# Eleven instead of seven products of zeros ahead of the first real matrix product

## The chip, the cores and the metric

The kernel runs on one NeuronCore of one Trainium2 chip. The metric is the device time of one execution in microseconds (us). The time before is the median of three executions, 374.33 us (373.33 to 376.72). Engines are named as the profile names them: PE is TensorE's matmul, PEld its load of the stationary operand, DVE is VectorE, ACT is ScalarE, POOL is GpSimd, and SP is SyncE, which issues most transfers.

## What is computed

The reference mixes two branches of one input x (1 x 2048 x 512) with a gate per row:

```python
g = sigmoid((x * gate_w).sum(-1, keepdims=True))
a = irfft2(rfft2(x) * (w_r + 1j * w_i))          # over both axes, 2048 x 512
b = gelu(x @ w1 + b1) @ w2 + b2                  # 512 -> 1792 -> 512
return g * a + (1 - g) * b
```

Everything is float32; both branches read the same x.

## The kernel before

**Tiling.** The 2048 rows are handled as 16 row groups of 128, and the 512 columns as four blocks of 128 (the index q in the code). The Fourier branch is a product with tables over columns (tiles pd), a product with tables over rows (py), vector butterflies, the filter, and the way back (pz, pa). The MLP runs over four blocks of 512 columns of transposed input (c) and two halves of the 14 hidden blocks (f): `ph` is the first layer's accumulator (12 products per hidden block: 4 blocks q times 3), `po` the second layer's.

**Split operands.** Each float32 operand of a real product is split into a high part and a low part (names ending in h and l: `wa0h`, `wa0l` for the first layer's weights of hidden block 0, `mxh`, `mxl` for the input, `g_0h`, `g_0l` for GELU's result, `wb0h`, `wb0l` for the second layer). ACT or DVE makes the high part as a rounded copy, DVE the low part as a difference. For some weights the low part is made in another way: ACT writes minus the high part (L557), and a transfer issued by POOL adds the raw weights from memory on top (L495). High times high, high times low and low times high are accumulated.

**Order.** Every piece of work is a step of a graph (`add`, with an engine, an estimated cost and a rank from a table). A planner (`Graph.schedule`) runs through the graph with these costs once, when the kernel is built, and so fixes the order of instructions on each engine. On the chip each engine works its list in order, and waits on semaphores for what it needs from the others.

**The start.** DVE clears a 128 x 128 tile `zero` (L568). PE then multiplies it with itself, as 128 x 512 products into a tile `none` that nobody reads (`warm`, through the helper `mm`, L504). In the meantime the first input blocks (`xf`) and first-layer weights (`war`) come from memory. ACT copies the first input block's high part in two halves (L637), DVE that of the second block (L639), the weights' first halves come from DVE (L1059) and ACT (L1057). The first eight real products are 128 x 128 wide and go to hidden block 0 (`ph`); then follow groups of four 128 x 256 wide products that alternate between hidden blocks 0 and 1, then the first Fourier products `pd`, which need ACT's `eoh` (L699), DVE's `eol` (L701) and the gate columns that DVE writes into the table `cf` (L612, L613). With its last product, hidden block 0 goes to ACT for GELU (L1125), then to `g_0h` (ACT, L551) and `g_0l` (DVE, L552).

The product of zeros, as the code gives it:

```python
zero, none = buf("hid", [P, P], F32R, "zero"), buf("pm", [P, 4, P], F32, "none", pool=pp)
mm(none.ap(), zero.ap(), bcast(zero.ap(), 4), True, True)
```

Of the kernel before, what the change touches and what calls it, by code (L numbers as in the profile page):

```python
# [264 lines left out]
class Graph:  # L265
# [5 lines left out]
    def add(self, eng, cost, lag, emit, reads=(), writes=(), rank=1):  # L271

        s = Step(len(self.steps), eng, cost, lag, emit, [], rank)
        deps = set()

        def parts(x):
            b, p = x if isinstance(x, tuple) else (x, None)
            if isinstance(b, View):
                return b.buf, range(b.lo, b.lo + b.n) if p is None else (b.lo + p,)
            return b, range(len(b.wrote)) if p is None else (p,)  # L280

        for x in reads:
            b, ps = parts(x)
            for p in ps:
                if b.wrote[p] is not None:
                    deps.add(b.wrote[p])
                b.read[p].append(s)
            if b not in s.bufs:
                s.bufs.append(b)
        for x in writes:  # L290
            b, ps = parts(x)
            for p in ps:
                if b.wrote[p] is not None:
                    deps.add(b.wrote[p])
                deps.update(b.read[p])
                b.wrote[p], b.read[p] = s, []
            if b not in s.bufs:
                s.bufs.append(b)
        deps.discard(s)
        for d in deps:  # L300
            d.after.append(s)
        s.need = s.open = len(deps)
        for b in s.bufs:
            b.left += 1
            if b.seq is None:
                b.seq = self.order.get(b.cls, 0)
                self.order[b.cls] = b.seq + 1
        self.steps.append(s)
        return s
# [125 lines left out]
def tile_kernel(ctx: ExitStack, tc: tile.TileContext, xt, xc, w1, w2, b1, b2, x0g, wf, wrev, out, consts):  # L435
# [10 lines left out]
    vec, act, pe, sp = nc.vector, nc.scalar, nc.tensor, nc.sync  # L446
# [7 lines left out]
    add = g.add  # L454

    def buf(tag, shape, dt=F32, name="", parts=1, pool=None, cls=None):
        slots.setdefault(tag, 1)
        return Buf(g, pool or (sb if tag in whole else sc), tag, shape, dt, name, parts, cls)
# [44 lines left out]
    def mm(ps, w, x, start, stop):  # L503
        pe.matmul(ps, w, x, start=start, stop=stop)  # L504
# [6 lines left out]
    def bcast(ap, *ns):  # L511
        return bass.AP(tensor=ap.tensor, offset=ap.offset, ap=[list(ap.ap[0]), *[[0, n] for n in ns], list(ap.ap[1])])
# [54 lines left out]
    zero, none = buf("hid", [P, P], F32R, "zero"), buf("pm", [P, 4, P], F32, "none", pool=pp)  # L567
# [3 lines left out]
      -1).table = "gelu"  # L571

    def warm():
        for _ in range(7):
            mm(none.ap(), zero.ap(), bcast(zero.ap(), 4), True, True)

    add("pe", 3.9, 0.1, warm, [zero], [none], 0)


    x0 = buf("ba", [P, NQ, P], F32, "xf0", parts=2)  # L580
# [718 lines left out]
```

## Time and profile before

| what | value |
|---|---|
| three executions | 373.33, 374.33, 376.72 us |
| the profiled execution's own time | 375.85 us |
| its span, first to last instruction | 374.0 us |
| instructions | 5583 |
| PE matmuls, of which products of zeros | 1850, 7 |
| transfers | 61.20 MB, mean 164 GB/s |

The profiled execution is 1.5 us longer than the median of the three; 1.85 us of its time lie outside its span. Busy shares in the profile are of the whole span; here only the first 50 us matter for the change, and those are read from the rows of the timeline and from the table by stretches. Times in rows count from the first instruction. Starts of products that follow each other are the measure of how fast PE works, since a product's own duration contains the pipeline behind it.

### The profile page before, as it was taken

What the parts mean: (1) busy time and instruction counts of PE and PEld (TensorE: products, weight loads), DVE (VectorE), ACT (ScalarE), POOL (GpSimd) and SP (SyncE); (2) the same over time, 40 slices, a digit from 0 to 9 for tenths busy, and PEclk for the clock granted to TensorE, in tenths of its full rate; (3) what the DMA queues carried; (4) which work ended last, traced back from release to release, by engine and by line L of the source; (5) the groups of instructions that cost most, each with busy time, mean ns of one, the idle gap of its engine ahead of it and who ended that gap; (6) DMA issues with size and microseconds to landing.
All of it is one profiled execution on the core that took longest, in us unless ns stands there. A gap on an engine that the chain in (4) does not pass through costs nothing.

```text
span 374.0 us, 5583 instructions
## 1 busy us (share of the span) xinstructions
PE 367.2 (98%) x1850; PEld 313.4 (84%) x1850; DVE 337.2 (90%) x745; ACT 225.7 (60%) x415; POOL 34.0 (9%) x54
## 2 busy tenths in 40 slices
PE   8999899999999999999999999999999999999996
PEld 6988788888888888888888888888888888888885
DVE  5799899999999999999999897789698999999982
ACT  4799757679935622357297429852964599544500
POOL 0023000000000000003024010100020000001110
PEclk9999999999999999999999999999999999999999
DMA  8999987286875153388778881325242053365456
GB/s 256 330 276 243 219 261 254 79 266 190 263 227 150 31 189 126 123 232 162 175 203 143 183 252 45 48 60 224 42 63 44 2 194 124 91 184 140 105 166 181
DMA packets 41909, 61.20 MB, mean 164 GB/s; under 512 B 4656, under 2 KB 22384, under 8 KB 41104
## 3 DMA queue, kind: packets, MB, share of 16 engines
q1 hardware_dynamic: 36120, 50.62, 42.4%
q0 software_dynamic: 5472, 9.96, 17.2%
q8 instruction: 14, 0.23, 0.3%
q10 hardware_dynamic: 288, 0.26, 0.2%
q14 instruction: 15, 0.12, 0.1%
HBM read 41.82 MB, written 16.92 MB: 157 GB/s over the span
## 4 chain that ended last, share of the span: by engine, by line
PE 89%; DMA 4%; ACT 3%; issue 1%; DVE 1%; POOL 0%; ACTq 0%; SPq 0%; POOLq 0%
PE po L504 40%; PE ph L504 38%; PE pz L504 4%; PE pa L504 3%; PE py L504 2%; PE pd L504 2%; DMA wb4l<-in_w 2%; DMA wbr<-in_w 1%; DMA xf<-in_x0g 1%; ACT ph L1125 1%; ACT eoh L699 0%; POOL wb3l L495 0%; DVE mxl L642 0%; ACT zb L740 0%; ACT wa6l L557 0%
## 5 line engine op out<-in xcount | busy, mean ns | idle before, releaser
L1125 ACT ACTIVATE ph<-ph,b1t 128x512 f32<-128x512 f32 x56 | 36.9, 658 | 51.0 <-PE ph L504 50.7
L958 ACT ACTIVATE sw<-y,al 64x512 f32<-64x512 f32 x32 | 22.8, 722 | 3.2 <-DVE y L821 2.6
L917 DVE TENSOR_TENSOR m<-y,wf 128x514 f32<-128x514 f32 x32 | 20.8, 689 | 0.1
L504 PE MATMUL py<-zb,tf 128*128 128x258 f32 x96 | 17.1, 287 | 0.0
L965 DVE SCALAR_TENSOR_TENSOR pq<-y,al,sw 128x256 f32<-128x256 f32 x32 | 14.5, 483 | 2.6 <-ACT sw L961 2.4
L773 ACT ACTIVATE y<-pys 64x257 f32<-64x257 f32 x32 | 13.4, 418 | 5.1 <-DVE pys L770 4.6
L504 PEld LDWEIGHTS py<-zb,tf 128*128 128x128 f32 x96 | 14.8, 190 | 1.4
L1164 ACT ACTIVATE o<-po,b2t 128x512 f32<-128x512 f32 x8 | 5.5, 688 | 16.3 <-PE po L504 16.3
L495 POOL DMA_DIRECT2D w<-ba x8 | 7.0, 873 | 77.8 <-ACT v4h L551 44.9
L504 PEld LDWEIGHTS pa<-zb,ci 128*128 128x128 f32 x96 | 13.0, 191 | 0.9
L694 DVE TENSOR_TENSOR w<-eo 128x256 f32<-128x256 f32 x32 | 13.2, 420 | 0.2
L742 DVE TENSOR_TENSOR zb<-pd,zb 128x256 fp32r<-128x256 f32 x32 | 12.6, 419 | 0.8 <-PE py L504 0.4
L504 PE MATMUL pa<-zb,ci 128*128 128x256 f32 x96 | 13.2, 283 | 0.0
L746 DVE TENSOR_TENSOR zb<-zb,pd 128x256 fp32r<-128x256 f32 (+1 forms) x32 | 12.8, 412 | 0.3
L691 DVE TENSOR_TENSOR eo<-xf 128x256 f32<-128x256 f32 x32 | 13.0, 419 | 0.0
L495 POOL DMA_DIRECT2D bacc<-o x8 | 7.0, 873 | 64.5 <-ACT o L1168 58.0
L740 ACT ACTIVATE zb<-pd 128x256 fp32r<-128x256 f32 x32 | 11.1, 382 | 2.5 <-PE pd L504 2.2
L495 POOL DMA_DIRECT2D wa7l<-in_w x1 | 0.9, 875 | 125.9 <-ACT wa7l L557 125.9
L701 DVE TENSOR_TENSOR eol<-w,eoh 128x512 fp32r<-128x512 f32 (+1 forms) x17 | 11.1, 655 | 1.2 <-ACT eoh L699 1.2
L986 DVE TENSOR_TENSOR zb<-pz,zb 128x512 fp32r<-128x512 f32 x16 | 11.0, 688 | 0.2
L988 DVE TENSOR_TENSOR zb<-zb,pz 128x512 fp32r<-128x512 f32 x16 | 11.0, 687 | 0.2
L1168 ACT ACTIVATE o<-po 128x512 f32<-128x512 f32 x8 | 4.7, 592 | 9.7 <-PE po L504 9.7
(558 smaller groups left out, 1309.9 us busy)
## 6 DMA issues: line engine op xcount, KB each, us to landing
wf<-in_wf SPq DMA_DIRECT2D x16, 257.0 KB, 3.5
bacc<-o SPq DMA_DIRECT2D x16, 256.0 KB, 3.2
xf<-in_xt SPq DMA_DIRECT2D x14, 256.0 KB, 4.9
wbr<-in_w SPq DMA_DIRECT2D x14, 256.0 KB, 4.5
war<-in_w SPq DMA_DIRECT2D x13, 256.0 KB, 3.1
xm<-in_xc SPq DMA_DIRECT2D x12, 256.0 KB, 4.8
tf<-tf SPq DMA_DIRECT2D x16, 192.0 KB, 4.3
bb<-bacc SPq DMA_DIRECT2D x8, 256.0 KB, 4.5
```

What stands on the lines that cost most here:

```text
L495: return add("pool", 2.3 * kb / 340, 3.4, lambda: nc.gpsimd.dma_start(dst(), src(), accum_op=ALU.add), reads, writes, rank)
L504: pe.matmul(ps, w, x, start=start, stop=stop)
L691: v(lambda s=s, op=op: vec.tensor_tensor(eo.ap()[:, s], x.ap()[:, 0:2], x.ap()[:, 2:4], op=op), 256, [x], [(eo, s)], feed)
L694: v(lambda s=s, op=op: vec.tensor_tensor(w.ap()[:, s], eo.ap()[:, :, 0], eo.ap()[:, :, 1], op=op), 256, [eo], [(w, s)], feed)
L701: v(lambda k=k: vec.tensor_tensor(l.ap()[:, k], w.ap()[:, k], h.ap()[:, k], op=ALU.subtract), 256 * len(ps), sub[0] + sub[1], sub[2], feed)
L742: v(lambda c=c: vec.tensor_tensor(segs(xl, c, 0, P + c), segs(ps, c, P, P + 4), segs(xh, c, 0, P + c), op=ALU.subtract), 256, [(ps, c), xh ...
L746: v(lambda o=o, i=i: vec.tensor_tensor(xl.ap()[:, :, o], xl.ap()[:, :, o], ps.ap()[:, :, i], op=ALU.add), 256, [ps], [xl], 0)
L773: a(lambda o=o, i=i: act.activation(Y[j].ap()[o:o + HP, 1], pys.ap()[i:i + HP, 1], AF.Copy), 257, [(pys, 1)], [(Y[j], 1 + k)], 0, more=0.1)
L917: v(lambda mk=mk, k=k, y=y, w=w: vec.tensor_tensor(mk.ap(), y.ap(), w.ap()[:, k:k + 1, :ND].to_broadcast([P, 2, ND]), op=ALU.mult), 514, [ ...
L958: a(lambda sw=sw, y=y, o=o, i=i: act.activation(sw.ap()[o:o + HP], y.ap()[i:i + HP, ::-1, :HD], AF.Copy, scale=al.ap()[i:i + HP, 0:1]), 51 ...
L965: v(lambda sw=sw, pq_=pq_, y=y, j=j, k=k, op=op: vec.scalar_tensor_tensor(pq_.ap()[:, k], y.ap()[:, k, :HD], al.ap()[:, 1 + j:2 + j], sw.a ...
L1125: a(lambda f=f, ps=ps: act.activation(ps.ap(), ps.ap(), AF.Gelu_apprx_tanh, bias=b1t.ap()[:, f:f + 1]), 600, [b1t], [ps], 0.9 if half else ...
```

## The change

`warm` issues eleven products of zeros instead of seven, and the cost by which the planner reckons this step rises from 3.9 to 4.35 us.

```diff
     def warm():
-        for _ in range(7):
+        for _ in range(11):
             mm(none.ap(), zero.ap(), bcast(zero.ap(), 4), True, True)
 
-    add("pe", 3.9, 0.1, warm, [zero], [none], 0)
+    add("pe", 4.35, 0.1, warm, [zero], [none], 0)
```

PE's list begins with the zeros, followed by the first products of hidden blocks 0 and 1. Before:

```order
L504 MATMUL none<-zero 128x512 x7
L504 MATMUL ph_0_132<-mxh_121,wa0h 128x128 x8
L504 MATMUL ph_0_132<-mxl_128,wa0h 128x256 x4
L504 MATMUL ph_1_172<-mxh_121,wa1h 128x256 x4
L504 MATMUL ph_1_172<-mxl_128,wa1h 128x256 x4
```

And now:

```order
L504 MATMUL none<-zero 128x512 x11
L504 MATMUL ph_0_136<-mxh_125,wa0h 128x128 x8
L504 MATMUL ph_0_136<-mxl_132,wa0h 128x256 x4
L504 MATMUL ph_1_176<-mxh_125,wa1h 128x256 x4
L504 MATMUL ph_1_176<-mxl_132,wa1h 128x256 x4
```

Only the count of the first row differs; the buffer numbers in names rise by four. The rest of PE's list and the lists of the four other engines, SP's and POOL's transfers among them, stand in the same order before and after: the planner's higher cost moves nothing.

## Prediction

> **What bounds the kernel now.** I read the shares and the chain first, then PE's waits, since the change adds work to PE's list alone.
>
> ```profile
> span 374.0 us, 5583 instructions
> PE 367.2 (98%) x1850; PEld 313.4 (84%) x1850; DVE 337.2 (90%) x745; ACT 225.7 (60%) x415; POOL 34.0 (9%) x54
> PE 89%; DMA 4%; ACT 3%; issue 1%; DVE 1%; POOL 0%; ACTq 0%; SPq 0%; POOLq 0%
> ...
> PE po L504 <- DMA wb4l<-in_w: 1.4, 1, 1.4
> PE none L504 <- DVE zero L568: 1.1, 1, 1.1
> PE ph L504 <- DVE mxh L639: 0.4, 1, 0.4
> PE ph L504 <- ACT mxh L637: 0.3, 1, 0.3
> ```
>
> PE is the bound, and it waits four times in 374 us (who <- for whom: total, times, longest). Three waits lie in the first 6 us, one of 1.4 us at 43.75, for the low part of a second-layer weight. Behind that PE never stops, so whatever time the change wins or loses must get past this one wait to reach the end. The start, in order of time:
>
> ```profile
> 1.09 3.35 PE L504 MATMUL none<-zero 128*128 128x512 f32 x7 [1.09 <-DVE zero L568]
> ...
> 4.75 0.69 PE L504 MATMUL ph<-mxh,wa0h 128*128 128x128 f32 x2 [0.30 <-ACT mxh L637]
> 5.88 1.54 PE L504 MATMUL ph<-mxh,wa0h 128*128 128x128 f32 x6 [0.44 <-DVE mxh L639]
> 7.22 1.16 PE L504 MATMUL ph<-mxl,wa0h 128*128 128x256 f32 x4
> ...
> 9.03 1.05 PE L504 MATMUL ph<-mxl,wa1h 128*128 128x256 f32 x4
> 9.89 1.05 PE L504 MATMUL ph<-mxh,wa0l 128*128 128x256 f32 x4
> ...
> 12.45 0.64 PE L504 MATMUL ph<-mxl,wa0h 128*128 128x256 f32 x4
> 12.93 0.64 PE L504 MATMUL ph<-mxh,wa0l 128*128 128x256 f32 x4
> ...
> 15.72 0.44 PE L504 MATMUL ph<-mxh,wa2h 128*128 128x512 f32 x1
> ```
>
> Four equal products take 9.89 - 9.03 = 0.86 us, 0.214 each, until about 12.45; after that 12.93 - 12.45 = 0.48, 0.120 each. **PE runs at about half speed up to 12.45 us.** The granted clock does not tell it: it reads 1.00 on both sides (the column ahead of the DMA share), while the matmuls in two microseconds go from 11 to 17.
>
> ```profile
> 10.00:12.00 2.00, 2.00 (x11) 2.00 (x11) 1.09 (x4) 1.18 (x3) 0.00 (x0) 1.00 0.94 327
> 12.00:14.00 2.00, 2.00 (x17) 2.00 (x16) 1.64 (x6) 0.39 (x1) 0.00 (x0) 1.00 0.96 308
> ```
>
> What ended the slow stage? From 1.09 PE worked 3.35 us on zeros, then paused twice (0.30 and 0.44 us); from 5.88 it did not pause, and 6.57 us later it was fast. So by these rows 3.35 us without a pause were not enough, and 6.57 were.
>
> [...]
>
> **The change, step by step.** Four more products of zeros. Their spacing:
>
> ```profile
> 1.68 1.05 PE L504 MATMUL none<-zero 128*128 128x512 f32 x2
> 3.39 1.05 PE L504 MATMUL none<-zero 128*128 128x512 f32 x2
> ```
>
> These rows begin with the second and the sixth: (3.39 - 1.68) / 4 = 0.4275. The seventh starts at 3.82, the eleventh at 5.53 and has streamed by **5.95** if PE is still slow: 4 x 0.43 = 1.71 us more on PE. Of that, 0.30 us filled the first pause and 0.44 the second. The first two real products, which started at 4.75, follow at 5.95 and end at 6.38; the next six could start at 5.88 and now start at 6.38. **So the direct price is 0.5 us**, all of it before PE's work is dense.
>
> The gain is that PE no longer pauses from 1.09 on. If zeros count as work, the fast stage comes after 4.44 (where 3.35 us had not sufficed) and by 1.09 + 6.57 = 7.66. Late end: zeros to 5.95, two and six products at 0.214 to 7.66, then eight groups of four at 0.48 complete hidden block 0 at 11.50. A product's result is out 0.16 us after its 0.12 (the row at 12.93: 0.64 for four, less three spacings, is 0.28 for one), so at 11.66. The three groups of hidden block 1 end at 12.94, four `pd` at 13.42, and four narrower ones 0.4 later (15.72 - 15.32 in the rows above and below) at 13.82. `ph` of block 2 starts there instead of at 15.72: PE gains 1.9. At the early end PE meets its inputs:
>
> ```profile
> 6.15 0.63 ACT L1063 ACTIVATE wa1h<-war 128x512 fp32r<-128x512 f32 x1 [0.27 <-DMA war<-in_w]
> 8.04 0.63 ACT L641 ACTIVATE mxh<-xf 128x512 fp32r<-128x512 f32 x1 [0.55 <-DMA xf<-in_xt]
> 8.41 1.28 DVE L642 TENSOR_TENSOR mxl<-xf,mxh 128x512 fp32r<-128x512 f32 x2
> 10.02 0.69 DVE L1065 TENSOR_TENSOR wa1l<-war,wa1h 128x512 fp32r<-128x512 f32 x1
> 11.27 0.40 ACT L699 ACTIVATE eoh<-w 128x256 fp32r<-128x256 f32 x1
> 12.24 0.17 DVE L613 TENSOR_TENSOR cf<-gg,cf 128x4 fp32r<-128x4 f32 x1
> 13.26 0.42 DVE L691 TENSOR_TENSOR eo<-xf 128x256 f32<-128x256 f32 x1
> 13.61 0.66 ACT L1125 ACTIVATE ph<-ph,b1t 128x512 f32<-128x512 f32 x1 [1.94 <-PE ph L504]
> 14.93 0.69 DVE L552 TENSOR_TENSOR g_0l<-ph,g_0h 128x512 fp32r<-128x512 f32 x1 [1.25 <-ACT g_0h L551]
> 15.32 0.56 PE L504 MATMUL pd<-cf,eol 128*128 128x130 f32 x4
> ```
>
> Up to 13.61 none of these waits for PE, so they stay. `cf` is ready at 12.41, so `pd` starts at about 12.45 at best, and block 2 at 13.33: PE gains at most 2.4. Block 0 is there by 11.66 in either case, and ACT is free at 11.67. **GELU moves from 13.61 to 11.67: 1.94 us on ACT.** Then `g_0l`, 1.32 us behind GELU, could start at 12.99, but DVE is busy until 13.26 + 0.42 = 13.68: **1.25 us on DVE.** Between 15 and 25 us both engines have no idle time to give up (the columns are PE, PEld, DVE, ACT, POOL):
>
> ```profile
> 15.00:20.00 5.00, 5.00 (x29) 4.29 (x28) 4.97 (x14) 4.89 (x11) 1.02 (x1) 1.00 1.04 343
> 20.00:25.00 5.00, 5.00 (x28) 4.27 (x27) 5.00 (x14) 4.94 (x11) 0.87 (x1) 1.00 1.07 306
> 35.00:40.00 5.00, 5.00 (x30) 4.41 (x29) 5.00 (x15) 4.92 (x13) 2.42 (x3) 1.00 0.77 187
> ```
>
> ACT and DVE feed each other there, so I take the smaller, 1.25, for both. It then has to get past the wait at 43.75 (the last row is that of the tile wb4l, from issue to landing):
>
> ```profile
> 34.04 0.63 ACT L557 ACTIVATE wb4l<-wb4h 128x512 fp32r<-128x512 f32 x1
> 35.02 0.86 POOL L495 DMA_DIRECT2D wb4l<-in_w  x1 [2.88 <-ACT wb4l L557]
> 41.93 0.40 PE L504 MATMUL po<-g_4l,wb4h 128*128 128x512 f32 x1
> 43.75 0.50 PE L504 MATMUL po<-g_4h,wb4l 128*128 128x512 f32 x1 [1.42 <-DMA wb4l<-in_w]
> DMA to landing us min/median/max: 8.7/8.7/8.7
> ```
>
> ACT's copy comes 1.25 earlier, so POOL issues the transfer at 33.8 and with the same 8.7 us it lands at 42.45. PE would be there 1.9 to 2.4 us earlier and wait about 0.65 to 1.15 us longer than now; the end moves by 1.25. The bounds are 0 (the transfer lands where it did) and 1.94 (ACT's gain passes whole).
>
> The sum against the profiled execution: 375.85 - 1.25 = 374.6. That execution is 1.5 us above the median, and may be one with a late fast stage. One in which it came 3.35 us after 5.88, at 9.23, the earliest that the rows leave open, has block 0 ready near 12.0: of the 1.25 on DVE nothing is left to win, on ACT 0.4. Between 0 and 1.25 I take 0.8, nearer to the one execution seen: 374.33 - 0.8 = **373.5 us**.
>
> **Rivals.** *Absorbed at the wait for wb4l.* The transfers are at 1.04 and 1.07 of their share between 15 and 25 us, and wb4l needs 8.7 us for 256 KB; if that is set by traffic and not by its issue, PE comes earlier and waits longer: 374.3. Against it: between 35 and 40, when wb4l is under way, the share is only 0.77.
>
> *Slower: zeros do not count.* If products of zeros do not end the slow stage, it ends where it did, counted from real work, and only the price is left: eight products 0.5 us late at 0.214. By 12.45 that is 2.3 products behind, which cost 0.28 at 0.120; if the fast stage itself comes 0.5 later, all of it. GELU, with nothing but PE ahead of it, passes it on: 374.33 + 0.4 = 374.7. It decides from the point where the last zero ends behind 5.88. For it: seven zeros did nothing that can be seen. Against it: they were shorter than the 6.57 us that worked.
>
> *More than forecast.* ACT's 1.94 reach the transfer: 374.33 - 1.94 = 372.4.
>
> *The moment is drawn anew.* The fast stage starts anywhere between 4.44 and 7.66, in each execution elsewhere. Then block 0 is still ready by 11.66, since both ends were worked out above, and the time is that of the forecast, 373.5; only the time before would differ between executions, as 373.33 to 376.72 may show. [...]
>
> That the change does something else than it says is excluded by the lists: all engines keep their order.
>
> **How the numbers follow.** Forecast 373.5: 0.54, of which 0.25 with a moment that is drawn anew. Absorbed, 374.3: 0.24. Slower, 374.7: 0.16. More, 372.4: 0.04. Something not seen, 0.02. The executions before spread from 1.0 below to 2.4 above their median, so a median of three is uncertain by about 1 us. The range takes the outer cases less part of that: 371.8 to 375.6. 1% is 3.7 us, about what a measurement here can tell from no change; no case gets there, and only a changed pattern of transfers or a disturbed median would: 0.03 faster, 0.04 slower, 0.93 within.
>
> **What would show it.** Right: the eleventh zero at about 5.5, no pause of PE between 1.1 and 40 us, a spacing of 0.120 before 8 us, GELU near 11.7, `g_0l` near 13.7, block 2 near 13.3 to 13.8, wb4l issued near 33.8 and PE's wait for it about 2.3 us. Absorbed: the same start, but wb4l lands at 43.7 still. Zeros do not count: spacing 0.214 until 9 us or later. I would be wrong if PE got a new wait behind 44 us, or if the start stays slow.

## The result and the profile after

| | before | after |
|---|---|---|
| median of 20 executions | 374.41 us (372.88 to 376.72) | 373.82 us (372.88 to 376.36) |
| ratio | | 0.9989, 95% interval 0.9971 to 1.0007 |
| a second comparison (17 and 12 executions) | 374.06 us | 373.68 us, 0.9989 (0.9968 to 1.0011) |
| profiled execution | 375.85 us | 376.36 us |

Both comparisons lie 0.1% below one, and neither interval excludes no change. The time is inside the predicted range, 0.3 us above the predicted 373.5. The profiled execution after happens to be the slowest of the twenty; its lines show why. First the page, PE's waits and PE's row of the start (the same views as before):

```profile
span 374.6 us, 5591 instructions
PE 367.8 (98%) x1854; PEld 312.7 (83%) x1854; DVE 337.3 (90%) x745; ACT 225.9 (60%) x415; POOL 33.9 (9%) x54
...
PE po L504 <- DMA wb4l<-in_w: 1.6, 1, 1.6
PE none L504 <- DVE zero L568: 1.1, 1, 1.1
PE ph L504 <- ACT mxh L641: 0.6, 1, 0.6
...
1.09 4.98 PE L504 MATMUL none<-zero 128*128 128x512 f32 x11 [1.09 <-DVE zero L568]
5.90 1.00 PE L504 MATMUL ph<-mxh,wa0h 128*128 128x128 f32 x8
6.74 0.73 PE L504 MATMUL ph<-mxl,wa0h 128*128 128x256 f32 x4
7.31 0.64 PE L504 MATMUL ph<-mxh,wa1h 128*128 128x256 f32 x4
9.47 0.75 PE L504 MATMUL ph<-mxh,wa1h 128*128 128x256 f32 x4 [0.56 <-ACT mxh L641]
11.70 0.64 ACT L1125 ACTIVATE ph<-ph,b1t 128x512 f32<-128x512 f32 x1
13.73 0.68 DVE L552 TENSOR_TENSOR g_0l<-ph,g_0h 128x512 fp32r<-128x512 f32 x1
13.80 0.44 PE L504 MATMUL ph<-mxh,wa2h 128*128 128x512 f32 x1
```

The two pauses before 6 us are gone, and the eight products of width 128 take 6.74 - 5.90 = 0.84 us: PE is fast from about 5.9 on instead of 12.45. GELU of block 0 comes at 11.70 instead of 13.61, `g_0l` at 13.73 instead of 14.93, block 2 at 13.80 instead of 15.72. Then the wait for wb4l and what follows it:

```profile
33.82 0.86 POOL L495 DMA_DIRECT2D wb4l<-in_w  x1 [2.88 <-ACT wb4l L557]
40.49 0.40 PE L504 MATMUL po<-g_4l,wb4h 128*128 128x512 f32 x1
42.45 0.50 PE L504 MATMUL po<-g_4h,wb4l 128*128 128x512 f32 x1 [1.56 <-DMA wb4l<-in_w]
43.52 0.63 PE L504 MATMUL po<-g_4h,wb4h 128*128 128x512 f32 x1
43.95 0.63 PE L504 MATMUL po<-g_4l,wb4h 128*128 128x512 f32 x1
DMA to landing us min/median/max: 8.6/8.6/8.6
```

The transfer is issued 1.20 earlier and PE goes on 1.30 earlier. But products of 512 columns now follow each other every 43.95 - 43.52 = 0.43 us, not every 0.23. The table by stretches says it in the granted clock, after and then before:

```profile
43.40:46.80 3.40, 3.40 (x11) 2.72 (x11) 1.47 (x6) 1.72 (x5) 0.00 (x0) 0.50 1.06 316
```

```profile
43.40:46.80 3.40, 3.05 (x17) 2.69 (x18) 1.92 (x6) 1.63 (x5) 0.00 (x0) 1.00 1.09 300
```

For 3.4 us PE is back at half speed, and by its end, at 46.73, it is 0.23 us behind the kernel before. **In this execution the win of the start (1.30 us at 42.45) was given back by a slow stage behind the wait (1.53 us).** Behind that the two traces run 0.23 to 0.5 us apart to the end. This is one execution; the experiments say how typical either profile is.

### The profile page after: what moved, and what is told of

It is laid out like the page before. It is cut to its first block, busy times and chain, and to the rows that moved or that the text cites. A ratio compares the mean times of both kernels' runs of the same rounds, so it can differ in the third digit from the quotient of the medians.

```text
span 374.6 us, 5591 instructions
## 1 busy us (share of the span) xinstructions
PE 367.8 (98%) x1854; PEld 312.7 (83%) x1854; DVE 337.3 (90%) x745; ACT 225.9 (60%) x415; POOL 33.9 (9%) x54
## 4 chain that ended last, share of the span: by engine, by line
PE 88%; DMA 4%; issue 3%; ACT 3%; POOL 1%; SPq 1%; DVE 0%; POOLq 0%; ACTq 0%
PE po L504 40%; PE ph L504 36%; PE pz L504 4%; PE pa L504 3%; PE py L504 3%; PE pd L504 2%; DMA wb4l<-in_w 2%; DMA xm<-in_xc 1%; DMA xf<-in_x0g 1%; ACT ph L1125 0%; ACT eoh L699 0%; POOL wb2l L495 0%; POOL wb3l L495 0%; POOL wa6l L495 0%; SPq L563 0%
```

## Experiments

Each kernel was compared with the kernel before on one chip. The order of all lists is that of the changed kernel except where an edit moves something.

### Profiles of the same kernels again

No edit. Three more profiles of the kernel before, and two more of the changed kernel, of which the first came with a comparison.

> The kernel before, a second profile. [...]

> [...]

> [...] With a granted clock of 0.995 the slow stage lies either near 8 us (behind an early fast stage) or behind the wait for wb4l at 43 us; with 1.000 there is one change alone, at the start.

> The changed kernel once more, unchanged, with its own comparison, since the gain (0.11% with an interval of 0.18% on either side) is below what the first comparison could tell. Theory A: ratio 0.997 to 0.9995, and the mean granted clock of an execution, which tells of a slow stage behind the first fast one, is 0.995 in fewer of its executions than of the kernel before (9 of 30 there, 1 of 20 here so far). The profile shows the fast stage beginning between 4.4 and 7.7 us, GELU of block 0 within 0.2 of 11.7 whatever this moment is, and PE's work behind wb4l beginning between 41.5 and 42.5. Rival G (the moment matters): GELU moves with it.

> The changed kernel, a third profile. Theory H: the fast stage begins anywhere from 4.0 to 7.7 us without a break behind it at the start, GELU of block 0 between 11.2 and 12.0, the issue of wb4l about 20 us behind g_0l, and PE's work behind wb4l begins between 41.2 and 42.5.

PE's list at the start, from the three profiles of the kernel before in turn, the third with its row of the table by stretches:

```profile
6.00 0.89 PE L504 MATMUL ph<-mxh,wa0h 128*128 128x128 f32 x6 [0.69 <-DVE mxh L639]
6.72 0.74 PE L504 MATMUL ph<-mxl,wa0h 128*128 128x256 f32 x4
9.81 0.75 PE L504 MATMUL ph<-mxh,wa1h 128*128 128x256 f32 x4 [0.91 <-ACT mxh L641]
```

```profile
9.34 0.74 PE L504 MATMUL ph<-mxh,wa1h 128*128 128x256 f32 x4 [0.58 <-ACT mxh L641]
```

```profile
5.86 0.88 PE L504 MATMUL ph<-mxh,wa0h 128*128 128x128 f32 x6 [0.69 <-DVE mxh L639]
6.59 0.74 PE L504 MATMUL ph<-mxl,wa0h 128*128 128x256 f32 x4
7.67 1.06 PE L504 MATMUL ph<-mxl,wa1h 128*128 128x256 f32 x4
8.53 1.05 PE L504 MATMUL ph<-mxh,wa0l 128*128 128x256 f32 x4
...
7.60:11.00 3.40, 3.40 (x18) 3.40 (x18) 3.23 (x10) 2.57 (x5) 0.00 (x0) 0.50 1.02 338
```

PE is fast with its second group of real products already: the six of width 128 take 0.72 us in the first of them (6.00 to 6.72) and 0.73 in the third (5.86 to 6.59), against 1.34 in the profile that the prediction read (5.88 to 7.22). In the second, too, PE is ahead of its inputs and waits for ACT before 9.34. So **seven zeros are often enough**; of these four profiles, the one on which the prediction stood is the exception (a fifth with seven zeros, of the last experiment, is fast only from 10.2 us). The first two do not lose the early fast stage again (mean granted clock 1.000). In the third of the new ones it is lost again for 3.4 us (granted clock 0.50 from 7.6 to 11.0), behind the two pauses that follow the zeros (0.34 and 0.69 us). The two profiled executions with one such lost stretch, this one and that of the changed kernel above, have a mean granted clock of 0.995. In the comparisons of these experiments 21 of 87 executions of the kernel before had 0.995, of the changed kernel 1 of 32 (its profiled execution above). Only that one and the third profile here show where the stretch lies; for the others it is inferred. These were not the slow executions: the median of the 21 is 373.7 us, that of the other 66 374.3, and three of the four comparisons have this order (in the other the two medians agree). So what the four added zeros save is hardly these stretches.

The three span 372.5, 372.2 and 371.4 us, the two more of the changed kernel 371.7 and 372.9. In the last two the start differs by the landing of an input block (xf), which ACT copies (L641): once PE does not wait for it, once it waits 1.74 us.

```profile
7.68 1.27 ACT L641 ACTIVATE mxh<-xf 128x512 fp32r<-128x512 f32 x2 [1.32 <-DMA xf<-in_xt]
11.23 0.66 ACT L1125 ACTIVATE ph<-ph,b1t 128x512 f32<-128x512 f32 x1
...
33.09 0.86 POOL L495 DMA_DIRECT2D wb4l<-in_w  x1 [2.88 <-ACT wb4l L557]
41.36 0.50 PE L504 MATMUL po<-g_4h,wb4l 128*128 128x512 f32 x1 [1.20 <-DMA wb4l<-in_w]
```

```profile
9.27 1.24 ACT L641 ACTIVATE mxh<-xf 128x512 fp32r<-128x512 f32 x2 [2.91 <-DMA xf<-in_xt]
12.78 0.66 ACT L1125 ACTIVATE ph<-ph,b1t 128x512 f32<-128x512 f32 x1
...
34.89 0.86 POOL L495 DMA_DIRECT2D wb4l<-in_w  x1 [2.88 <-ACT wb4l L557]
42.34 0.50 PE L504 MATMUL po<-g_4h,wb4l 128*128 128x512 f32 x1 [0.35 <-DMA wb4l<-in_w]
```

The second block's copy is the last input of block 0 from ACT. It begins one copy (0.63 us) ahead of the end of its row, at 8.32 in the first and at 9.88 in the second, and GELU follows 2.91 and 2.90 us behind it; in the first profile of the changed kernel and in the first two new ones of the kernel before it is 2.91 or 2.92. So GELU is not within 0.2 of 11.7, as theory A had it: what sets it is this landing, not the moment at which PE became fast (5.9 and 5.5 us). The 41.36 of the first lies just ahead of the expected 41.5 to 42.5, the 12.78 of the second behind the expected 11.2 to 12.0. Neither of these two has a slow stage behind wb4l.

### No zeros, five zeros

```diff
-        for _ in range(11):
+        for _ in range(0):
```

> The products of zeros are left out altogether; every list is otherwise that of the changed kernel. Theory A (zeros help only if they join the real work without a pause; seven did not): the first real products start near 3.9 us, pause until about 5.9 as before, the fast stage comes no earlier than about 9.2 us, GELU of block 0 between 12.0 and 13.7, PE's wait for wb4l 1.3 to 1.6 us, and the time is that of the kernel before within 0.3 us (374.1 to 374.7). Rival B (each product of zeros warms a little): fast stage later than 12.5 and time 375 or more. Rival C (the start does not reach the end, the transfer of wb4l lands when it lands): 374.4 as well, but with PE's wait for wb4l short where block 0 was late.

The five-zero kernel has `range(5)`.

> Five products of zeros instead of seven or eleven, nothing else. The profiles of the kernel before showed a fast stage from 4.2 to 4.6 us in three of four executions, so seven zeros (PE busy 1.1 to 4.4 us) are enough when the moment falls well. [...] Rival B (each product of zeros helps a little): between 374.1 and 374.4, with a clock of 0.995 in some.

Without zeros 374.71 us, ratio 1.0007 (0.9990 to 1.0023); with five 374.93 us, 1.0011 (0.9988 to 1.0033). The profiles are slow until about 9.8 and 11.2 us, the latter shown here, where the spacing changes inside the group at 10.73:

```profile
4.74 0.69 PE L504 MATMUL ph<-mxh,wa0h 128*128 128x128 f32 x2 [1.15 <-ACT mxh L637]
5.87 1.54 PE L504 MATMUL ph<-mxh,wa0h 128*128 128x128 f32 x6 [0.44 <-DVE mxh L639]
...
9.88 1.05 PE L504 MATMUL ph<-mxh,wa0l 128*128 128x256 f32 x4
10.73 0.84 PE L504 MATMUL ph<-mxh,wa1h 128*128 128x256 f32 x4
11.40 0.65 PE L504 MATMUL ph<-mxh,wa0h 128*128 128x256 f32 x4
```

Without zeros two expectations of theory A are missed: the first real product starts at 4.83 us and not near 3.9, and PE waits only 0.85 us for wb4l, not 1.3 to 1.6. GELU lies inside the 12.0 to 13.7 that were expected without zeros in both profiles (12.49 and 13.05). None of the 24 executions had a granted clock of 0.995. Five zeros do no more than none, which speaks against a little help by each. The whole effect from none to eleven is some 0.2%, and neither a single step of it nor the whole is clear of the intervals.

### 32 zeros

```diff
-        for _ in range(11):
+        for _ in range(32):
```

> 32 products of zeros instead of 11, nothing else. At 0.427 us until the fast stage (4.4 to 7.7 us) and 0.22 behind it they end at about 10.4 to 11.8 us, so everything that waits for the first real products is 3 to 5 us later than with eleven: GELU of block 0 at 15.2 to 16.6, g_0l about 1.4 later. Theory A (what the start wins or loses on DVE and ACT reaches wb4l and the end nearly whole): wb4l is issued 2.5 to 3.9 us later than with eleven, at about 36.3 to 37.7, and the time is 376.5 to 378. Rival C (the wait for wb4l absorbs it): wb4l lands where it landed, near 42.5 to 43.8, PE's wait there disappears, and the time is 373.5 to 374.8.

377.52 us, ratio 1.0090 (1.0055 to 1.0125). The first real products come at 10.23 us, GELU at 15.16, and:

```profile
16.49 0.69 DVE L552 TENSOR_TENSOR g_0l<-ph,g_0h 128x512 fp32r<-128x512 f32 x1 [2.03 <-ACT g_0h L551]
36.60 0.86 POOL L495 DMA_DIRECT2D wb4l<-in_w  x1 [2.87 <-ACT wb4l L557]
46.11 0.80 PE L504 MATMUL po<-g_4h,wb4l 128*128 128x512 f32 x1 [2.21 <-DMA wb4l<-in_w]
DMA to landing us min/median/max: 9.5/9.5/9.5
```

The wait for wb4l did not absorb the delay: wb4l was issued 20.11 us behind `g_0l`, as in the changed kernel (33.82 - 13.73 = 20.09). Theory A holds (GELU came 0.04 us ahead of its expected range), rival C falls. In this execution PE's wait of 2.21 us was followed by two slow stretches, and it took 381.27 us, the longest of its seven:

```profile
45.80:49.20 3.40, 3.09 (x10) 2.79 (x11) 0.17 (x1) 0.77 (x2) 0.00 (x0) 0.50 1.02 297
49.20:52.60 3.40, 3.40 (x10) 2.66 (x9) 2.81 (x9) 1.47 (x3) 0.00 (x0) 0.50 0.33 108
```

### Filling the wait

```diff
...
+                            for _ in range(fill.pop()):
+                                mm(ps.ap(), calm[0], gl[:, n], False, False)
                             mm(ps.ap(), wl[:, s], gh[:, n], False, f == fs[-1])
```

`calm` is a tile of zeros, cleared by DVE next to `zero`, and `fill` holds the number 8, once: the edit applies to the first product that reads wb4l. The dots stand for the lines around it.

> The changed kernel with eight products of a tile of zeros put ahead of the first product that reads wb4l, where PE waits; they add zero to the sum. PE is then busy for 1.8 us of the wait. Theory D (a wait of 1.5 us at wb4l can halve PE's clock for the next 3.4 us, when enough of it falls together): the profile shows no slow products behind the wait and granted clock 1.00 there in any execution, and where the wait is over 1.8 us nothing is lost. If the slow stage was rare, the median stays within 0.3 us of the changed kernel's 373.8; if it comes in many executions, the median falls by up to 1.5 us. Rival E (the slow stage behind the wait has another cause, such as the transfers): it appears here too.

374.53 us, ratio 1.0020 (0.9999 to 1.0042), 0.7 us above the 373.8 within 0.3 that was expected. No execution of twelve had 0.995, but one of 32 without the fill had it, so this tells little of the cause (D or E). The fill itself was too long: wb4l landed 7.9 us behind an issue at 34.25, at 42.2, and PE was at the eight products until 43.03. Far behind it, in the same profile, PE waited 0.8 us for another weight's transfer (wa13l); whether the fill has to do with it is open.

```profile
34.25 0.86 POOL L495 DMA_DIRECT2D wb4l<-in_w  x1 [2.88 <-ACT wb4l L557]
41.17 2.02 PE L504 MATMUL po<-g_4l,calm 128*128 128x512 f32 x8
43.03 0.39 PE L504 MATMUL po<-g_4h,wb4l 128*128 128x512 f32 x1
```

### Taking the wait away

Two ACT instructions, wb4h and wb4l (steps 597 and 598), move ahead of zb and g_5h, to directly behind wb3l (step 587), or, in the second kernel, only behind g_5h (step 613):

```diff
     order = g.schedule()
+    early_w = [s for s in order if s.n in (597, 598)]
+    order = [s for s in order if s.n not in (597, 598)]
+    k = [s.n for s in order].index(587) + 1
+    order[k:k] = early_w
```

> The changed kernel with two ACT instructions, wb4h and wb4l of the fifth second-layer weight, moved ahead by six places, directly behind wb3l; nothing else moves. POOL issues the transfer of wb4l about 2.5 us earlier, near 31.3 us. Theory A (this wait is the gate behind which the start's gain is lost or kept): PE's wait at wb4l falls from 1.56 us to under 0.3, PE goes on near 41 us instead of 42.45, and the time falls by 1.0 to 1.5 us below the changed kernel, to 372.3 to 372.8. Rival C (the transfers' traffic sets the landing): wb4l takes 2.5 us longer from issue to landing, PE waits as before, and the time stays at 373.8. Rival F (ACT's delayed pieces, zb and g_5h, bring a new wait of PE): PE waits ahead of 41 us, and the time stays within 0.5 of 373.8.

> The changed kernel with wb4h and wb4l on ACT moved ahead by three places, behind g_5h, instead of six, so that zb and g_5h stay where they are. Theory A: wb4l is issued about 1.6 us earlier, near 31.5 to 32.2, lands near 40, and PE, which is there at 39.8 to 40.5, waits under 0.5 us instead of 1.2 to 1.6, with no new wait ahead; time 372.4 to 373.0 against 373.7. Rival C: the transfer takes as much longer as it is issued earlier; 373.7. Rival F: the eoh and y pieces that are now later on ACT cost PE a new wait; 373.5 to 374.

By six places: 373.70 us, 0.9993 (0.9973 to 1.0012), no better than the changed kernel. The wait at wb4l is gone, but PE has a new one for DVE's `g_5l`, which is rival F:

```profile
PE ph L504 <- DVE g_5l L552: 0.6, 1, 0.6
```

The transfer, issued at 30.57, landed after 5.3 us, and not later by what it was issued earlier, so rival C falls. That the new wait is why the time did not fall isn't shown: the profiled execution is one of the faster (373.14 us), and PE reaches wb4l at 41.19 in it, as in the next kernel.

By three places: **373.10 us, 0.9961 (0.9942 to 0.9980)**, clear of no change and the fastest kernel here by its median, 0.1 above the expected 372.4 to 373.0. PE has no wait at wb4l and no new one; all that are left lie at the start:

```profile
PE ph L504 <- ACT mxh L641: 1.3, 1, 1.3
PE none L504 <- DVE zero L568: 1.1, 1, 1.1
PE ph L504 <- DVE mxh L639: 0.3, 1, 0.3
...
32.55 0.86 POOL L495 DMA_DIRECT2D wb4l<-in_w  x1 [1.34 <-ACT wb4l L557]
41.16 0.39 PE L504 MATMUL po<-g_4h,wb4l 128*128 128x512 f32 x1
```

wb4l lands 6.7 us behind its issue, at 39.3, and PE reaches it at 41.16 without a pause, although the input block was late in this execution (GELU at 12.50).

### The same move with seven zeros

The last edit, in the kernel before.

> The kernel before, with seven zeros, and the same two ACT instructions moved by three places as in the fast variant with eleven zeros (373.1 us, ratio 0.9961). It tells how much of that variant's gain belongs to the zeros. Theory H (four more zeros only save the executions in which seven fell badly; the rest of the gain is the wait for wb4l): 373.3 to 373.9, ratio 0.997 to 0.9985, and a granted clock of 0.995 in about a quarter of its executions. Rival (the move needs the early start): 374.2 or more. Rival (the zeros are worth nothing once the wait is gone): 373.1 within 0.15.

373.19 us, 0.9977 (0.9957 to 0.9997). Against 0.9961 with eleven zeros the intervals overlap widely: with the wait gone, four more zeros are worth too little to be told here (0.09 us by the medians). Theory H's 373.3 is missed by 0.1, its ratio is met, and 0.995 came in one of twelve executions and not in a quarter; the rival's 373.1 within 0.15 is met; the two can't be told apart. In the profile PE is slow until 10.2 us, and yet it reaches wb4l without a wait, at nearly the same time as with eleven zeros (41.16), and the span is the same (371.6 us):

```profile
12.67 0.66 ACT L1125 ACTIVATE ph<-ph,b1t 128x512 f32<-128x512 f32 x1 [0.28 <-PE ph L504]
41.23 0.39 PE L504 MATMUL po<-g_4h,wb4l 128*128 128x512 f32 x1
```

With eleven zeros PE was fast from 4.7 us on, but then waited 1.3 us for the late input block, and GELU came at 12.50.

## Why the prediction was right, and where it was not

- **No pause, an early fast stage.** Right for the two old pauses and the fast stage; a new pause of 0.56 us came ahead of 9.47. The eleventh zero started at 5.52, the spacing was 0.12 from 5.9 on. Zeros do count as work: PE was fast right behind the eleven at 5.90 us, and behind 32 the first eight real products took 0.84 us (10.23 to 11.07), as fast as here, so the slower rival fell. The rival that the moment is drawn anew holds in so far as the moment differed between executions, though with a lower end below 4.44: PE was fast from 4.2 us on in one execution with seven zeros and from 4.0 in one with eleven. What makes it differ, no run shows.
- **The price of 0.5 us.** Too high for that execution. The first two products moved from 4.75 to 5.90, as worked out (5.95), but the other six, already fast, lost 0.19 at their first and were ahead from the third on.
- **1.94 on ACT, 1.25 on DVE.** 1.91 and 1.20. But "up to 13.61 none of these waits for PE, so they stay" holds for one trace only: the block that ACT copies at 8.04 there was copied at 8.3 to 9.9 in the profiles of the changed kernel, and GELU followed it. An early PE then waits at 9 us.
- **The gate at wb4l.** Right in size: 1.20 earlier at the issue, 8.6 us to landing, 1.30 at PE. The 32 zeros show the same in the other direction. The other profiles bear the gate out: in ten of the fourteen, 330.2 to 330.5 us pass from PE's first product with wb4l to the end, and the other four have a slow stage or a later wait for wa13l behind it. But "the same 8.7 us" was luck: without the move of ACT's instructions and with up to eleven zeros, the transfer took 7.4 to 8.7 us, so the landing moves by as much as the start was to win. PE's own lead had shrunk from 1.92 to 1.44 us by 40.49, so its wait grew to 1.56 and not to about 2.3; what took the 0.48 us, in small steps behind 30 us, was not found.
- **Between 0 and 1.25, taken as 0.8.** Measured 0.6 us by the first medians, 0.4 by the second. The direction may be right; it isn't shown, since both intervals hold no change. The step behind it failed: "3.35 us without a pause were not enough" was drawn from one execution. Three of four profiles of the kernel before have the fast stage from before 6 us on (three of five with seven zeros), so many executions had little or nothing left to win, and the earliest moment, 9.23, was no bound. That the forecast lies 0.3 us from the measured time is in part luck: 0.8 was a choice between 0 and a gain worked out from an execution that was not the common one.
- **A new loss behind the wait.** Not foreseen: I wrote that the wait would be longer, and not that PE may be slow behind a longer wait. It cost 1.53 us in one profile; of 32 executions one had the clock of 0.995 that goes with it. Of the ten profiles with a wait at wb4l, the two with over 1.5 us (1.56 and 2.21) have a slow stage there and the eight with 0.2 to 1.4 us have none. That the wait is its cause is argued from this, not shown.

What stays open: how much of the 0.4 to 0.6 us comes from a late first fast stage, since only profiled executions show when it begins, and how much from chance. The lost stretches (21 of 87 executions before) hardly explain it, as said above.

## What to carry to other kernels

One profile shows one execution. Where a moment differs between executions of the same kernel, as here between 4.2 and 12.4 us, take several profiles of the kernel before, and count how often the costly case comes, before a change is built on it. Work done earlier is worth what passes the next wait: here the wait for one weight's low part decided more than the start, and moving two ACT instructions by three places brought 0.2% with seven zeros and 0.4% together with four more, while the four products of zeros alone brought about 0.1% that can't be told from nothing.

## What the hardware showed

The moment at which PE becomes fast differed between executions of the same kernel. By the traces' records of the granted clock it was 12.4, 4.6, 4.5 and 4.2 us in the kernel before, 5.8, 5.9 and 5.5 in the changed one; without zeros 9.8, with five 11.2, with seven and the moved instructions 10.2, and 4.0 to 4.9 in the other kernels with eleven or more. The slow stages behind a first fast one, at a granted clock of 0.50, lasted 3.4 us (7.6 to 11.0, and 43.4 to 46.8) or, with 32 zeros, twice that (45.8 to 52.6). What sets the moment and these lengths, no run shows.

Pauses of about the same length came with a slow stage and without one. PE paused 1.56 us at wb4l and was at half clock from 43.4; and in the third new profile of the kernel before, the slow stage came behind pauses of 0.34 and 0.69 us among eight narrow products. No slow stage came behind 1.20 us in another execution, nor behind 1.42 in the first profile, nor behind 0.42 and 0.69, or 0.29 and 0.69, in the first two new ones, nor behind the 1.74 us for the late input block in the last profile of the changed kernel. No run placed a pause on purpose, and what decides it stays open.

The granted clock read 1.00 in the stage ahead of the first change, though products were about half as fast there (1.00 from 10 to 12 us before, at 0.214 us from product to product, against 0.120 from 12.45 on); behind it, a slow stage read 0.50 (43.4 to 46.8 after, at 0.43 us against 0.23). At the start the spacing of products has to be read instead.
